# A middle part one step later on ScalarE, a lower part on GpSimd, and GpSimd's constants in another order

## The chip, the cores and the metric

The kernel runs on one core of a Trainium2 chip. A core has five engines that run their own instruction queues and meet only at semaphores: TensorE (PE in the profile, with its weight loads as PEld), VectorE (DVE), ScalarE (ACT), GpSimd (POOL) and SyncE (SP), which here issues nearly all transfers. Work on each engine is done in the order in which the program lists it: an instruction that waits holds up everything behind it on that engine. The metric is the device time of one execution in microseconds (us). Times are given to 0.01 us where they come from the trace.

## The reference: what is computed

Two independent results stand side by side in the output, each of 2048 rows and 576 columns.

The left half is attention with a compressive memory. With `x` of 2048 x 576, the projections `q = x wq`, `k = x wk`, `v = x wv` are cut into 32 heads of 18 columns and four segments of 512 rows. In each segment:

```
logits = qs ks^T * scale + causal mask
a_dot  = softmax(logits) vs
a_mem  = (phi(qs) M) / (phi(qs) z + 1e-6)      phi(t) = t + 1 for t > 0, else exp(t)
o      = g a_mem + (1 - g) a_dot               g = sigmoid(beta), one per head
M += phi(ks)^T vs ;  z += sum of phi(ks)       carried to the next segment
```

The four segments' `o`, put together, are multiplied by `wo`.

The right half is a Fourier mixing layer by matrices: `a = x Hr^T`, `b = x Hi^T` over the 576 columns, and `y = Cr a - Ci b` over the 2048 rows.

## The kernel before, in words

**Numbers in parts.** Products are not made in plain float32. A float32 operand is cut into an upper part (a rounded copy, made by ScalarE) and a lower part (the operand minus its upper part, made by VectorE or GpSimd), and the product is the sum of upper x lower, upper x upper and lower x upper. In the code `split`, `split_wk`, `split_x` and `c_cut` do this. The projected queries and keys are cut into three bfloat16 parts: `p0` is a copy of the PSUM result (ScalarE, L275), `r` the remainder (VectorE, L276), the middle part `p1` a copy of `r` (L285 on GpSimd for the key tiles 5, 6 and 7, L287 on ScalarE for all others) and the last part `p2` the remainder of that (GpSimd, L288).

**Stages.** Stage 1 runs over the four segments (`for s in range(NSEG)`). For each segment it makes nine tiles of 128 rows of projected queries and keys (`project_qk`, in the order m = 0, 1, 2, 3, 8, 4, 5, 6, 7; m = 0 to 3 are queries, 4 to 7 keys, 8 is half and half) and then, for each of four row blocks j, the values (`project_v`). In segments 0 to 2 `project_v` also turns the key tiles by TensorE transposes (`k_natural`, L305) so that they can be summed into the memory (`accumulate`). The transposes read a float32 copy of each key tile, `KF[m]`, which ScalarE makes first thing in `project_qk` (L271). In segments 1 to 3 `lookup` reads the memory. Its last two instructions are VectorE's `w` (L415) and GpSimd's `am` (L417); GpSimd's `vs` (L336) follows. The tiles `am` and `vs` leave by transfers `amd<-am` and `vd<-vs` of SP's queue.

Stage 2 mixes the 32 x 4 attention heads with the Fourier product. `attention()` is a generator of 68 steps (p) of eight slots each. After every slot the loop pulls as many pieces of the generator `dense()` as keep the two in proportion, by given unit costs. `dense()` starts with `hidden`, sixteen products of one chunk of the Fourier input each: `c_load` fetches chunk n to `craw` (four buffers), `c_cut` makes its upper part `chi` and the upper part of its last 128 rows, `xtail`, on ScalarE (L451, L453) and the lower parts `clo` and `xtail` on GpSimd (L456, L458). At the end of the last segment of stage 1 the first two chunks are cut by VectorE instead. Stage 3 is the product with `wo`.

**Order.** What runs when is written out by hand. `later(n, fn)` puts a call off by n ticks, and `tick()` is called after each tile, block or slot. What is due in a tick runs in the order in which it was put off. The middle and last part of a tile are such a call (`rest`), and the transfer of its three parts is put off by one tick more:

```
        def rest():
            if m in (5, 6, 7):
                pool.tensor_copy(p1, r)
            else:
                act.activation(p1, r, AF.Copy)
            pool.tensor_tensor(p2, r, p1, OP.subtract)
            if m < 8:
                later(1, dma, (qd if m < 4 else kd)[s][(m % 4) * P:(m % 4 + 1) * P, :3], p)
```

Buffers matter too. The parts `p` have five buffers, shared with `am`; the remainders `r` have three; a PSUM tile of stage 1 has five. Two TensorE instructions of stage 2 that the change touches by what stands ahead of them are `s` (scores, L965), which needs the PSUM bank that VectorE's row minima (L971) read before, and `trm` (L1022), which turns the row maxima that GpSimd packs into `mb` (L1015 to L1018, `maxima`). `maxima` stands behind the lower part of chunk 5 in GpSimd's order.

**Small tiles.** `attention_constants` makes, on GpSimd, the causal mask (L479, L480), which the row minima read, and clears the two `mb` tiles (L483). `stacks` makes a pair of key and query stacks; its only instruction is GpSimd's memset of ones in the last rows of the key stack (L466). There are four pairs: number 0 is made at the last segment's key tiles, number 1 after j = 1 of its values, and numbers 2 and 3 at the start of attention's steps 0 and 1. `stack_load` fills them by transfers of 432 KB each (`ks<-kd`, `qs<-qd`).

Of the kernel before, what the change touches and what calls it, by code (L numbers as in the profile page):

```python
# [40 lines left out]
def infini_attention_and_fnet(ctx: ExitStack, tc: tile.TileContext, xT, wqk, w8, wv, wo, beta, xtT, cT, hT, out):  # L41
    nc = tc.nc
    act, dve, pool, pe = nc.scalar, nc.vector, nc.gpsimd, nc.tensor
# [44 lines left out]
    def later(n, fn, *a):  # L88
        due.setdefault(clock[0] + n, []).append((fn, a))
# [173 lines left out]
    def project_qk(s, m):  # L263
        if m in FIRST:
            o = FIRST.pop(m)
        else:
            o = ps.tile([P, L], F32, name="qk", tag="acc", bufs=5)
            chain(o, qk_terms(s, m))
        if m >= 4 and s < 3:
            KF[m] = sk.tile([P, L], F32, name="kf", bufs=5)  # L270
            act.activation(KF[m], o, AF.Copy)  # L271
        p = sb.tile([P, 3, L], BF16, name="p", tag="p", bufs=5)
        r = sb.tile([P, L], F32, name="r", tag="r", bufs=3)
        p0, p1, p2 = (p[:, 2 - i] if 4 <= m < 8 else p[:, i] for i in range(3))
        act.activation(p0, o, AF.Copy)  # L275
        dve.tensor_tensor(r, o, p0, OP.subtract)  # L276
        if s and (m < 4 or m == 8):
            n = P if m < 4 else 64
            c = m if m < 4 else 4
            e = sb.tile([P, L], F32, name="qe", bufs=2)[:n]  # L280
            phi(e, ((e, o[:n]),), pq_hi[:n, c], pq_lo[:, c] if m < 4 else pq_hi[64:, c])
# [10 lines that stand above are left out]
                later(1, dma, qd[s][4 * P:, :3], p[:64])  # L292
                for i in range(3):
                    later(1, dma, kd[s][4 * P:, 2 - i], p[64:, i])

        later(1, rest)

    def k_natural(j):
        js = slice(j * P, (j + 1) * P)
# [144 lines left out]
    def c_cut(n, engine=pool):  # L444
        if n < len(CHUNKS):
            raw = c_raw.pop(n)
            hi = sr.tile([P, 4, P], F32R, name="chi", bufs=3)
            lo = sr.tile([P, 4, P], F32R, name="clo", bufs=3)
            t = sr.tile([P, P], F32R, name="xtail", bufs=3) if CHUNKS[n][2] == 5 else None
            c_split[n] = hi, lo, t  # L450
            act.activation(hi, raw[:, :4], AF.Copy)  # L451
            if t is not None:
                act.activation(t, raw[:, 4], AF.Copy)  # L453

            def low():
                engine.tensor_tensor(lo, raw[:, :4], hi.bitcast(F32), OP.subtract)  # L456
                if t is not None:
                    engine.tensor_tensor(t[64:], raw[64:, 4], t[64:].bitcast(F32), OP.subtract)  # L458
            later(1, low)
# [3 lines left out]
    def stacks(p_, i):  # L463
        qs_bufs.append(p_.tile([P, 4, L], BF16, name=f"qs{i}"))
        ks_bufs.append(p_.tile([P, 4, L], BF16, name=f"ks{i}"))
        pool.memset(ks_bufs[i].bitcast(F32)[96:], BF16_ONES)  # L466
# [10 lines left out]
    def attention_constants():  # L477
        t = CAUSAL[0]
        pool.memset(t, 0.0)  # L479
        pool.affine_select(t[:, 384:], t[:, 384:], pattern=[[-1, P]], base=0, channel_multiplier=1,  # L480
                           compare_op=OP.is_ge, fill=LOWEST)
        for m in MB:
            pool.memset(m, 0.0)  # L483
# [16 lines left out]
    for s in range(NSEG):  # L500
        more = s < 3
        if s == 0:
            warm_up()
        open_qk(s)
        if s:
            memory()
        else:
            tick()
        for n, m in enumerate((0, 1, 2, 3, 8, 4, 5, 6, 7)):
            project_qk(s, m)  # L510
            tick()
            if not more and n in (5, 7):
                h_split(0, (n - 5) // 2)
            if s and n < (8 if more else 4):
                copy_parts(s - 1, 2 * n)
                copy_parts(s - 1, 2 * n + 1)
            if s in (1, 2) and n >= 4:
                load_x(s + 1, n - 4)
            if not more and n == 0:
                for k in range(5):  # L520
                    h_load(0, k)
            if not more and n == 4:
                p1k.close()
                sr = ctx.enter_context(tc.tile_pool(name="sb2r", bufs=1, side="right", reuse_waits="tile"))
                attention_tiles()
            if not more and n == 4:
                c_load(0)
                c_load(1)
                stacks(sr, 0)
                stack_load(0)  # L530
            if not more and n == 6:
                c_load(2)
        for j in range(4):
            project_v(s, j, lookup(s, j) if s else iter(()))
            tick()
            for k in ((0, 1), (2, 3), (4,), ())[j] if s == 0 else ():
                load_x(1, k)
            if more and j in (1, 2):
                split_x(s + 1, j - 1)
            if not more and j == 1:  # L540
                stacks(sr, 1)
            if not more and j == 2:
                attention_constants()
            if not more and j == 0:
                h_split(0, 2)
                h_split(0, 3)
            if not more and j == 1:
                h_split(0, 4)
                c_cut(0, dve)
                c_cut(1, dve)  # L550
            if not more and j in (1, 3):
                c_load(3 + j // 2)
            if more and j:
                accumulate(j - 1)
# [393 lines left out]
    sq = ctx.enter_context(tc.tile_pool(name="sb2q", bufs=1, side="right", reuse_waits="tile"))  # L948
# [196 lines left out]
    def attention():  # L1145
        for p in range(NP + V_LAG):
            def even(lag, fn, *a):
                if 0 <= p - lag < NP:
                    fn(2 * (p - lag), *a)

            def odd(lag, fn, *a):
                if 0 <= p - lag < NP:
                    fn(2 * (p - lag) + 1, *a)

            if p < 2:
                stacks(sq, p + 2)
                OG.append(sa.tile([P, 4, 72], F32, name=f"og{p}"))
            if p == 0:
                value_load(0)
                stack_load(1)  # L1160
            if p % 2 == 0:
                later(39, value_load, p // 2 + 1)
                later(30, memory_load, p // 2)
            even(T_LAG + 1, t_lo, 0)
            odd(F_LAG + 1, f_exp, 2)
            odd(F_LAG + 1, f_split_hi)
            yield SLOTS[0]
            G = p // 2 - 1 if p % 2 == 0 and 0 < p <= NP else None
            even(0, s_fill, 0)
            even(T_LAG, t_fill, 0)  # L1170
            even(T_LAG, t_fill, 1, G)
            if G is not None and p < T_LAG:
                maxima_transpose(G, bank("trm", [P, L], F32, "t"))
            odd(F_LAG + 1, f_split_lo, pool, 512, 1280)
            yield SLOTS[1]
            even(0, s_fill, 1)
            odd(F_LAG + 1, f_split_lo, dve, 0, 512)
            yield SLOTS[2]
            even(V_LAG, pv)
            even(0, s_fill, 2)  # L1180
            even(T_LAG, t_mask)
            yield SLOTS[3]
            odd(F_LAG, f_fill, 1)
            even(T_LAG, t_fill, 2)
            odd(F_LAG, f_fill, 0)
            if p % 2 and p < NP:
                maxima(p // 2)
            yield SLOTS[4]
            odd(F_LAG + 1, f_turn)
            if p % 2:  # L1190
                stack_load((p + 3) // 2)
                if p < 16:
                    later(2, copy_parts, 2, 8 + p // 2)
            elif 4 <= p < 36:
                later(2, copy_parts, 3, (p - 4) // 2)
            even(T_LAG, t_hi)
            yield SLOTS[5]
            odd(V_LAG, pv)
            odd(F_LAG, f_fill, 2)
            odd(F_LAG, f_exp, 1)  # L1200
            even(T_LAG, t_lo, 1)
            even(T_LAG, t_lo, 2)
            yield SLOTS[6]
            odd(F_LAG, f_exp, 0)
            if V_LAG <= p < NP + V_LAG - 1:
                pv_out(p - V_LAG)
            yield SLOTS[7]
# [74 lines left out]
```

## Time and profile before

| | |
|---|---|
| median of three runs | 993.6 us (992.38 to 993.71) |
| the profiled execution | 991.08 us, of which 989.4 us are the span of its instructions |
| TensorE busy | 980.1 us, 99% of the span |
| VectorE, ScalarE, GpSimd busy | 790.1 us, 714.6 us, 674.0 us |
| stage 1 | to about 218 us |
| stage 2 (attention and Fourier product) | to about 933 us |

How to read the rows of this profile. A timeline row has the start, the time from the first start to the last end, the engine, the line, the operation, what is written and read, and how many instructions it merges. A bracket at the end gives the engine's idle time just before the row and what ended it. TensorE's matmuls are pipelined and their ends are modelled, so the time that a wait cost TensorE is better read from start to start than from the bracket. In the chain of waits a row has start, length and what the time was spent on. In a table of stretches there is the time, and for each engine its busy time with the number of instructions, then the granted clock, the busy share of the transfer engines and the rate in GB/s.

### The profile page before, as it was taken

Reading aid. Unit: us, or ns where it says so; the run is one execution under the profiler, and the core shown is the slowest. Engines: PE = TensorE matmul, PEld = TensorE weight load, DVE = VectorE, ACT = ScalarE, POOL = GpSimd, SP = SyncE. Lnnn points to the kernel's source line nnn. Section 1 sums busy time; section 2 is a strip of 40 time slices with the busy share of each in tenths; the row PEclk is TensorE's granted clock in tenths of the full one; section 3 lists DMA queues with packets and bytes.
Section 4 is the critical chain, followed back from the end, with each engine's and each line's share of the span. In section 5 each row is a group of like instructions: output and inputs, shape, how many; then the busy total and the mean of one; then the engine's idle time right before and its main releaser. Section 6 shows DMA issues by size and latency. Waiting matters only on the chain.

```text
span 989.4 us, 25491 instructions
## 1 busy us (share of the span) xinstructions
PE 980.1 (99%) x9246; PEld 918.0 (93%) x9246; DVE 790.1 (80%) x2115; ACT 714.6 (72%) x1687; POOL 674.0 (68%) x744
## 2 busy tenths in 40 slices
PE   9999999999999999999999999999999999999998
PEld 8989989898999999999999999999999999999998
DVE  6657668594678787887898887888889899999885
ACT  7757576663888777877878788886777877778442
POOL 2657576686676667676775777767677986667561
PEclk9999999999999999999999999999999999999999
DMA  7537456767577899899999987789999999888663
GB/s 252 188 116 251 185 179 241 238 236 216 147 182 205 225 235 236 199 235 232 226 260 229 236 210 195 183 196 219 234 240 263 229 243 242 206 206 190 168 199 114
DMA packets 304350, 209.96 MB, mean 212 GB/s; under 512 B 204992, under 2 KB 259136, under 8 KB 304192
## 3 DMA queue, kind: packets, MB, share of 16 engines
q1 hardware_dynamic: 304000, 208.20, 80.5%
q8 instruction: 72, 1.18, 0.5%
q14 instruction: 54, 0.44, 0.2%
q10 hardware_dynamic: 224, 0.14, 0.0%
HBM read 122.37 MB, written 58.98 MB: 183 GB/s over the span
## 4 chain that ended last, share of the span: by engine, by line
PE 83%; DVE 8%; ACT 4%; issue 2%; DMA 1%; POOL 1%; SPq 0%; POOLq 0%; DVEq 0%; ACTq 0%
PE d L583 37%; PE s L965 7%; PE v L84 4%; PE pv L1083 4%; PE qk L250 4%; PE d L628 3%; PE d L629 3%; PE d L630 3%; PE t L865 2%; PE pv L1084 2%; PE d L865 2%; PE s L865 1%; PE m L363 1%; PE t L1039 1%; PE qk L84 1%
## 5 line engine op out<-in xcount | busy, mean ns | idle before, releaser
L971 DVE CUSTOM_DVE_ANT_0 s<-s,causal 128x128 f32<-128x128 f32 (+3 forms) x512 | 248.1, 503 | 89.5 <-PE s L965 80.0
L456 POOL TENSOR_TENSOR clo<-craw,chi 128x512 fp32r<-128x512 f32 x158 | 218.0, 1380 | 86.1 <-ACT chi L451 59.6
L583 PE MATMUL d<-wide,chi 128*128 128x288 f32 x1408 | 261.8, 303 | 0.0
L583 PEld LDWEIGHTS d<-wide,chi 128*128 128x128 f32 x1408 | 210.7, 188 | 2.2 <-issue 0.7
L583 PE MATMUL d<-wide,clo 128*128 128x288 f32 x704 | 173.3, 313 | 0.0
L1005 POOL TENSOR_TENSOR hl<-pf,hl 128x768 f16<-128x768 f32 x64 | 112.3, 1755 | 64.5 <-ACT hl L1001 54.6
L1051 ACT ACTIVATE phi<-t 128x384 f16<-128x384 f32 x128 | 61.8, 483 | 102.0 <-PE t L1048 102.0
L965 PE MATMUL s<-ks,qs 108*128 108x128 bf16 (+3 forms) x512 | 132.8, 303 | 2.3 <-DVE negm L971 1.6
L994 ACT ACTIVATE pf<-s,nb 128x128 f32<-128x128 f32 (+3 forms) x256 | 128.3, 527 | 6.2
L1066 DVE TENSOR_TENSOR plo<-pf,phi 128x384 f16<-128x384 f32 (+1 forms) x128 | 128.5, 1004 | 0.0
L583 PE MATMUL d<-ab,chi 128*128 128x288 f32 x640 | 123.3, 302 | 0.0
L583 PEld LDWEIGHTS d<-wide,clo 128*128 128x128 f32 x704 | 117.8, 189 | 1.9 <-issue 0.4
L1052 ACT ACTIVATE pf<-t 128x384 f32<-128x384 f32 (+1 forms) x192 | 99.6, 519 | 6.2 <-PE t L1039 6.0
L451 ACT ACTIVATE chi<-craw 128x512 fp32r<-128x512 f32 x160 | 100.1, 626 | 3.6 <-DMA craw<-xtT 2.0
L583 PEld LDWEIGHTS d<-ab,chi 128*128 128x128 f32 x640 | 97.9, 189 | 0.5
L1001 ACT ACTIVATE hl<-pf 128x768 f16<-128x768 f32 (+1 forms) x128 | 87.4, 729 | 2.0
L583 PE MATMUL d<-ab,clo 128*128 128x288 f32 x320 | 83.0, 308 | 0.0
L628 PE MATMUL d<-wide,chi 128*128 128x288 f32 x256 | 81.4, 318 | 0.0
L630 PE MATMUL d<-wide,clo 128*128 128x288 f32 x256 | 75.6, 295 | 0.9 <-POOL clo L456 0.9
L629 PE MATMUL d<-wide,chi 128*128 128x288 f32 x256 | 75.6, 295 | 0.0
L1066 POOL TENSOR_TENSOR plo<-pf,phi 128x384 f16<-128x384 f32 x64 | 62.4, 974 | 14.9 <-ACT pf L1052 14.5
L1005 DVE TENSOR_TENSOR hl<-pf,hl 128x512 f16<-128x512 f32 x64 | 66.6, 1041 | 0.0
(285 smaller groups left out, 2522.6 us busy)
## 6 DMA issues: line engine op xcount, KB each, us to landing
craw<-cT SPq DMA_DIRECT2D x128, 256.0 KB
ks<-kd SPq DMA_DIRECT2D x32, 432.0 KB
qs<-qd SPq DMA_DIRECT2D x32, 432.0 KB
craw<-xtT SPq DMA_DIRECT2D x32, 320.0 KB
vd<-vs SPq DMA_DIRECT2D x16, 440.0 KB
vst<-vd SPq DMA_DIRECT2D x32, 220.0 KB
qd<-p SPq DMA_DIRECT2D x16, 384.0 KB
kd<-p SPq DMA_DIRECT2D x16, 384.0 KB
```

The lines of the kernel that those rows point to most:

```text
L451: act.activation(hi, raw[:, :4], AF.Copy)
L456: engine.tensor_tensor(lo, raw[:, :4], hi.bitcast(F32), OP.subtract)
L583: pe.matmul(o[h], a, b[:, h * 288:h * 288 + 288], start=start, stop=stop)
L628: pe.matmul(o, xh[:, k], wl[k][:, cs], start=k == 0, stop=False)
L629: pe.matmul(o, xh[:, k], wh[k][:, cs], start=False, stop=False)
L630: pe.matmul(o, xl[:, k], wh[k][:, cs], start=False, stop=False)
L965: pe.matmul(o[:, c:c + w], q[:, i * P:w], k[:, :w], start=True, stop=True)
L971: dve.tensor_tensor_reduce(o[:, c:c + w], o[:, c:c + w], CAUSAL[0][:, L - w:], scale=scale, scalar=-LOWEST, op0=OP.add, op1=OP.min, accum_ ...
L994: act.activation(f[:, FIRST_COL[i]:FIRST_COL[i] + w], o[:, c:c + w], AF.Exp, bias=nb[:, i:i + 1], scale=-1.0)
L1005: engine.tensor_tensor(hl[:, 1, a:b], f[:, a:b], hl[:, 0, a:b], OP.subtract)
L1052: act.activation(f[:, r:r + w], o[:, :w], AF.Exp, bias=LIFT, scale=SCALE)
L1066: (pool if kind == 2 else dve).tensor_tensor(lo[:, a:b], f[:, a:b], hi[:, a:b], OP.subtract)
```

## The change

Four edits. In segments 1 and 2 the middle and last part of key tile 4 (the first key tile proper) are put off by two ticks and not one, so they stand behind the copies of key tile 5. In the last segment `attention_constants` and the second pair of `stacks` change places (j = 1 and j = 2). The lower part of the second Fourier chunk is made by GpSimd and not by VectorE. The pairs 2 and 3 of `stacks` are made in the fourth slot of attention's steps 0 and 1, and not in their first.

```
-        later(1, rest)
+        later(2 if m == 4 and s in (1, 2) else 1, rest)
...
             if not more and j == 1:
+                attention_constants()
+            if not more and j == 2:
                 stacks(sr, 1)
-            if not more and j == 2:
-                attention_constants()
...
             if not more and j == 1:
                 h_split(0, 4)
                 c_cut(0, dve)
-                c_cut(1, dve)
+                c_cut(1, pool)
...
             if p < 2:
-                stacks(sq, p + 2)
                 OG.append(sa.tile([P, 4, 72], F32, name=f"og{p}"))
...
             yield SLOTS[2]
             even(V_LAG, pv)
+            if p < 2:
+                stacks(sq, p + 2)
             even(0, s_fill, 2)
```

More of the change, by code (lines that the diff above doesn't have):

```diff
@@ L294, in rest @@
                     later(1, dma, kd[s][4 * P:, 2 - i], p[64:, i])
-        later(1, rest)
+        later(2 if m == 4 and s in (1, 2) else 1, rest)
     def k_natural(j):
@@ L540, in infini_attention_and_fnet @@
             if not more and j == 1:
+                attention_constants()
+            if not more and j == 2:
                 stacks(sr, 1)
-            if not more and j == 2:
-                attention_constants()
             if not more and j == 0:
@@ L549, in infini_attention_and_fnet @@
                 c_cut(0, dve)
-                c_cut(1, dve)
+                c_cut(1, pool)
             if not more and j in (1, 3):
@@ L1155, in attention @@
             if p < 2:
-                stacks(sq, p + 2)
                 OG.append(sa.tile([P, 4, 72], F32, name=f"og{p}"))
@@ L1179, in attention @@
             even(V_LAG, pv)
+            if p < 2:
+                stacks(sq, p + 2)
             even(0, s_fill, 2)
```

## The prediction

> **What bounds the kernel now.** I read the page first, then the busy time by stretches, then the chain of waits, and last the rows engine by engine where TensorE stands. The last row here is from the table of stretches, the others from the page.
>
> ```profile
> span 989.4 us, 25491 instructions
> ...
> PE 980.1 (99%) x9246; PEld 918.0 (93%) x9246; DVE 790.1 (80%) x2115; ACT 714.6 (72%) x1687; POOL 674.0 (68%) x744
> ...
> PE 83%; DVE 8%; ACT 4%; issue 2%; DMA 1%; POOL 1%; SPq 0%; POOLq 0%; DVEq 0%; ACTq 0%
> ...
> 220.00:240.00 20.00, 17.98 (x133) 17.21 (x131) 10.56 (x36) 7.66 (x20) 11.78 (x16) 1.00 0.75 223
> ```
>
> TensorE is busy for 99% of the span and is 83% of the chain that ended last. Nothing else bounds the kernel for long, so a change gains only what TensorE now waits. In 220 to 240 us, where stage 1 passes into stage 2, it stands 20.00 - 17.98 = 2.02 us, more than in any other stretch of that length before the last one; the change is made around there and at two short waits before it.
>
> The first short waits are those of the transposes in segments 1 and 2 (TensorE's rows; the last one is a row of the chain of waits from a place where nothing was late):
>
> ```profile
> 86.20 0.60 PE L305 MATMUL kt<-ident,kf 128*128 128x128 f32 x4
> 87.00 0.33 PE L305 MATMUL kt<-ident,kf 128*128 128x128 f32 x1 [0.20 <-ACT kf L271]
> 87.31 0.45 PE L396 MATMUL look<-md,pq_hi 128*128 128x152 f32 x2
> ...
> 142.98 0.60 PE L305 MATMUL kt<-ident,kf 128*128 128x128 f32 x4
> ...
> 144.04 0.45 PE L396 MATMUL look<-md,pq_hi 128*128 128x152 f32 x2
> ...
> 163.12 0.55 PE kt L305 x5
> ```
>
> Five transposes and the start of what follows take 87.31 - 86.20 = 1.11 us in segment 1 and 144.04 - 142.98 = 1.06 us in segment 2, where undisturbed ones take 0.55 us: 0.56 + 0.51 = 1.07 us are lost, to ScalarE's copies of the key tiles.
>
> The later waits of TensorE, at the passage:
>
> ```profile
> 221.63 0.38 PE L965 MATMUL s<-ks,qs 108*128 108x128 bf16 x2 [0.31 <-DVE nd L407]
> 223.90 0.27 PE L965 MATMUL s<-ks,qs 108*128 108x256 bf16 x1 [0.83 <-DVE negm L971]
> 229.04 0.41 PE L630 MATMUL d<-wide,clo 128*128 128x288 f32 x1 [0.88 <-POOL clo L456]
> 241.29 0.23 PE L1022 MATMUL trm<-ident,mb 128*128 128x128 bf16 x1 [0.23 <-POOL mb L1018]
> ```
>
> Two of them end with VectorE, two with GpSimd; the brackets of the first three add to the 2.02 us.
>
> **The change part by part.**
>
> *Key tile 4, a step later.* ScalarE in segment 1, with one row each of VectorE (the remainder of tile 6) and GpSimd (last parts of tiles 8 and 4):
>
> ```profile
> 82.47 0.58 ACT L275 ACTIVATE p<-qk 128x512 bf16<-128x512 f32 x1
> 83.88 0.63 ACT L287 ACTIVATE p<-r 128x512 bf16<-128x512 f32 x1 [0.83 <-DVE r L276]
> ...
> 86.32 0.62 ACT L271 ACTIVATE kf<-qk 128x512 f32<-128x512 f32 x1
> ...
> 86.56 0.69 DVE L276 TENSOR_TENSOR r<-qk,p 128x512 f32<-128x512 f32 x1 [0.28 <-ACT p L275]
> ...
> 84.31 2.29 POOL L288 TENSOR_TENSOR p<-r,p 128x512 bf16<-128x512 f32 x2
> ```
>
> The middle part of tile 4 (83.88) waits 0.83 us for its remainder, and behind it stand the copies of tiles 5, 6 and 7, the last at 86.32. From 83.88 to 86.32 there are five starts of 0.49 us each. With the copy and upper part of tile 5 ahead of the middle part, the six starts from 82.47 follow without a gap and the last copy begins at 82.47 + 6 x 0.49 = 85.41. It ends by 86.0; TensorE gets to the fifth transpose at 86.20 + 4 x 0.11 = 86.64. So 0.56 us go here and 0.51 us in segment 2.
>
> What is late next: the lookup after the transposes needs the bank that the remainder of tile 6 reads. That remainder waits for its upper part (now about 85.5) and for the remainder buffer of tile 8, free when GpSimd's first last part ends (84.31 + 1.15 = 85.46). It runs from 85.6 to 86.3; the lookup stands at 86.75. The remainder of tile 7 needs the buffer of tile 4, free at 84.31 + 2.29 = 86.60, and ends near 87.3; the product that needs its bank comes 0.6 us after that. On GpSimd the order stays (tile 4's last part still ahead of tile 5's parts) and the queue is full, so nothing moves. On SP's queue tile 4's transfer is moved past two copies and one load, about 2.2 us; this costs nothing while `am` of the second row block, which takes over the buffer, comes later than the landing (the slower rival). Sum: -1.07 us, bounds -1.07 and 0. I take the first, since every next wait has 0.4 us or more in hand.
>
> All engines of segment 3 start from TensorE's last sums, so I shift them all by 1.07 us up to 216 us.
>
> *The second chunk's lower part, mask and ones.* VectorE, then GpSimd, then SP's transfer, the chain of waits behind it, and who waits for the load:
>
> ```profile
> 216.64 0.68 DVE L456 TENSOR_TENSOR clo<-craw,chi 128x512 fp32r<-128x512 f32 x1
> 217.35 1.15 DVE L458 TENSOR_TENSOR xtail<-craw,xtail 64x128 fp32r<-64x128 f32 x1
> 218.53 1.64 DVE L456 TENSOR_TENSOR clo<-craw,chi 128x512 fp32r<-128x512 f32 x1
> 220.19 0.42 DVE L458 TENSOR_TENSOR xtail<-craw,xtail 64x128 fp32r<-64x128 f32 x1
> 220.63 0.82 DVE L327 TENSOR_TENSOR vr<-v,vs 128x288 f32<-128x288 f32 x2
> ...
> 222.97 0.19 DVE L415 TENSOR_TENSOR w<-look,g 128x32 f32<-128x32 f32 x1
> ...
> 218.31 1.31 POOL L336 TENSOR_TENSOR vs<-vr,vs 128x576 bf16<-128x576 f32 x1
> 219.57 0.52 POOL L479 MEMSET causal<- 128x512 f32 x1
> ...
> 223.30 1.16 POOL L417 TENSOR_TENSOR am<-nd,w 128x576 f32<-128x576 f32 x1 [2.54 <-ACT xtail L453]
> 224.42 1.27 POOL L336 TENSOR_TENSOR vs<-vr,vs 128x576 bf16<-128x576 f32 x1
> 226.68 0.95 POOL L466 MEMSET ks<- 32x1024 f32 x1 [0.99 <-DMA amd<-am]
> 227.72 1.27 POOL L456 TENSOR_TENSOR clo<-craw,chi 128x512 fp32r<-128x512 f32 x1
> 229.07 0.46 POOL L458 TENSOR_TENSOR xtail<-craw,xtail 64x128 fp32r<-64x128 f32 x1
> ...
> 225.71 0.32 SPq L94 DMA_DIRECT2D vd<-vs  x1
> ...
> 228.50 8.99 DMA craw<-xtT
> ...
> 237.58 0.63 ACT L451 ACTIVATE chi<-craw 128x512 fp32r<-128x512 f32 x1 [2.03 <-DMA craw<-xtT]
> ...
> 238.34 1.28 POOL L456 TENSOR_TENSOR clo<-craw,chi 128x512 fp32r<-128x512 f32 x1 [4.00 <-ACT chi L451]
> ```
>
> VectorE loses 220.63 - 218.53 = 2.10 us of work ahead of `vr`. So `vr` begins at 218.5 - 1.07 = 217.45 and `w` ends at 217.45 + (223.16 - 220.63) = 219.98, 3.2 us sooner. The bank of the wait at 221.63 and the minima behind the wait at 223.90 come about as much sooner, TensorE 1.07 and 1.4 us sooner: both waits go. The mask, read by the minima, would now come too late behind the chunk; made before `am` and `vs` of block 2, in the time in which GpSimd made the ones, it is there at 215.5.
>
> GpSimd gets the chunk: after `vs` of block 2 (ends 219.57 - 1.07 = 218.50) come `clo` and `xtail`, 229.07 - 227.72 = 1.35 and about 0.5, so 1.85 us, then the ones of pair 1, 1.0 us, to 221.35. Only then `am` of block 3 can begin, though `w` has been ready since 219.98: it ends at 222.5 and `vs` at 222.5 + 1.27 = 223.77, against 225.69 before. That is 1.92 us sooner, 0.85 more than the shift. Nothing covers these 2.85 us of GpSimd's but the 2.54 us in which it stood idle before 223.30; what is over, 1.37 us past `w`, is paid here. Bounds: VectorE's 1.64 us for the same operation, overlapped with GpSimd's work, shows that the two can hold each other up; were GpSimd's 1.27 stretched as far, 0.4 us of the 1.92 would go. I take 1.27, what GpSimd's own rows have (227.72, 238.34), since VectorE runs `vr` and the lookup's short sums then.
>
> [...]
>
> *The ones of pairs 2 and 3 later.* The memset at 226.68 waits for the landing of `am` and holds up chunk 2's `clo`, for which TensorE waits at 229.04. After the change `clo` follows `vs` at once: 223.8 to 225.1, and TensorE, by then 1.07 + 0.31 + 0.83 = 2.2 us early, asks at about 225.8. The wait goes. The two memsets (0.95 us each) now stand ahead of chunk 3's and chunk 5's lower parts; GpSimd stands idle 4.00 us before the latter (238.34). From chunk 2 to chunk 5 TensorE takes 241.29 - 229.04, or 4.1 us a chunk; it asks for chunk 3 at about 225.8 + 4.1 = 229.9, and GpSimd has it by 225.6 + 0.95 + 1.27 = 227.8. Cost nothing; without that cover 0.95 us each.
>
> *What is late next.* After these, TensorE is 1.07 + 2.02 = 3.09 us early. But at 241.29 it waits for `mb`, which stands in GpSimd's order behind chunk 5, whose upper part waits on ScalarE (237.58) for the load issued at 228.50 and landed 8.99 us later. That load is in SP's queue behind `vd<-vs`, at 225.71 right after `vs`, and behind the loads of a chunk, of values, keys and queries, on transfer engines busy for 0.75 of the stretch. This whole row shifts with `vs`: by 1.92 us and no more. So at `trm` TensorE stands again, 3.09 - 1.92 = 1.2 us longer than the 0.23 us of before, and keeps 1.92 us. From there on every engine is early by the same, and the order of the work does not change.
>
> Sum: -1.07 (transposes) - 0.85 (`vs` of block 3, passed on through the load) = -1.92 us. The profiled execution took 991.08 us and would take 989.16; that execution lies 2.5 us under the median of the three runs, 993.6, so in terms of the median I predict 991.7 us.
>
> **The rivals.**
>
> Full gain: the load of chunk 5 doesn't set the end at `trm`, for instance because it lands sooner when the loads ahead of it are spread. For it speaks that only the last part of that transfer can be as late as 8.99 us; against it that those engines are busy (0.75) and that ScalarE did wait for it (2.03 us). Then all waits go, 1.07 + 2.02 + 0.23 = 3.3 us: 990.3 us.
>
> Half gain: GpSimd loses what VectorE wins, because `clo`, the ones and `am` take 0.85 us longer in their new place. For it speaks that GpSimd has only 2.54 us idle for 2.85 us of work. Then the transposes remain: 992.5 us.
>
> Slower: tile 4's transfer lands late. SP's rows, and `am` of the second row block:
>
> ```profile
> 89.90 0.38 SPq L94 DMA_DIRECT2D kd<-p  x1
> ...
> 91.65 0.62 SPq L109 DMA_DIRECT2D raw<-xT  x1
> 92.38 0.60 SPq L94 DMA_DIRECT2D kd<-p  x1
> ...
> 99.51 1.49 POOL L417 TENSOR_TENSOR am<-nd,w 128x576 f32<-128x576 f32 x1 [1.33 <-ACT xh L59]
> ```
>
> The transfer goes from 89.90 to about 92.0, just ahead of tile 5's. `am` takes its buffer at 99.51 - 0.56 = 98.95. The mechanism decides from a landing later than 6.9 us after the issue; the copies about it in that queue are of a kind that took long above (8.99 us). Each us more holds up GpSimd, the lower part of the keys behind `am` and TensorE's sums. With 2 us in both segments it costs 4 us: 991.7 + 4 = 995.7 us. Against it: the load that now goes ahead of it was itself issued at 91.65 and nothing waited.
>
> **How the numbers follow.** The forecast, gain of 1.92 us less the 0.4 us of the stretched `clo` or plus as much, has 0.60; its own range is 991.2 to 992.2. Full gain 0.20, half gain or none 0.11, slower 0.09. About 0.2%, here 1.99 us, is what a measurement of this kernel can tell from no change, that is 991.6 us. The forecast lies on that bound; the three runs spread over 1.3 us, and the small waits on VectorE in stage 2 can only shrink when work comes sooner, so I give 0.35 of its 0.60 to faster and 0.25 to the same. Faster: 0.35 + 0.20 = 0.55. Same: 0.25 + 0.11 = 0.36. Slower: 0.09. The range from 990.1 (full gain, a little past it) to 993.4 leaves out the slower case, no gain, and the runs beyond the full gain.
>
> **What would show each step.** Right: five transposes of 0.55 us in segments 1 and 2; no 0.83 us before the middle part; `vr` straight behind `xtail` on VectorE; no idle time of TensorE at 221 to 229; `vs` of block 3 about 1.9 us sooner; TensorE's wait for `mb` at `trm` longer by 1.2 us or more. Wrong: `trm` without a wait (full gain), `am` of block 3 no sooner than 1.07 us (half gain), GpSimd waiting for `kd<-p` before `am` (slower).

## The result, and the profile after

The changed kernel takes 989.55 us (median of 14 executions, 987.1 to 992.54), the kernel before 992.46 us (14 executions, 990.45 to 994.17). The ratio is 0.9973, with a 95% interval of 0.9961 to 0.9985: 2.7 us faster, between 1.5 and 3.9. The forecast gain of 1.92 us lies in that interval; the forecast time, 991.7 us with a range down to 990.1, does not fit. One further execution of the changed kernel took 3261.85 us and is left out of every comparison.

The profiled execution of the changed kernel took 992.54 us, the slowest of its 14. By its profile alone the change would look like a loss, and what makes it slow turned out to be the most instructive part of the case. First the head lines of its page (span; busy time, share and instructions of each engine):

```profile
span 990.8 us, 25491 instructions
...
PE 980.7 (99%) x9246; PEld 919.5 (93%) x9246; DVE 785.6 (79%) x2113; ACT 713.9 (72%) x1687; POOL 676.7 (68%) x746
```

VectorE has lost 4.5 us of work and GpSimd gained 2.7 us. TensorE is busy 0.6 us longer with the same 9246 matmuls, which is the first sign that something made matmuls slower.

The timeline of the kernel after, TensorE's rows only (start, length, engine, line, operation, out<-in, count, and idle time with its releaser):

```profile
86.90 0.71 PE L305 MATMUL kt<-ident,kf 128*128 128x128 f32 x5
87.36 0.43 PE L396 MATMUL look<-md,pq_hi 128*128 128x152 f32 x2
...
143.02 0.71 PE L305 MATMUL kt<-ident,kf 128*128 128x128 f32 x5
143.48 0.43 PE L396 MATMUL look<-md,pq_hi 128*128 128x152 f32 x2
...
220.57 0.39 PE L965 MATMUL s<-ks,qs 108*128 108x128 bf16 x2
221.87 0.28 PE L965 MATMUL s<-ks,qs 108*128 108x256 bf16 x1
...
237.51 0.39 PE L965 MATMUL s<-ks,qs 108*128 108x512 bf16 x1
240.76 0.23 PE L1022 MATMUL trm<-ident,mb 128*128 128x128 bf16 x1 [2.86 <-POOL mb L1018]
...
241.54 0.30 PE L630 MATMUL d<-wide,clo 128*128 128x288 f32 x1
241.68 0.30 PE L628 MATMUL d<-wide,chi 128*128 128x288 f32 x1
...
242.20 0.44 PE L628 MATMUL d<-wide,chi 128*128 128x288 f32 x1
242.44 0.44 PE L629 MATMUL d<-wide,chi 128*128 128x288 f32 x1
...
246.38 0.80 PE L965 MATMUL s<-ks,qs 108*128 108x256 bf16 x4
```

and two rows of TensorE before that were not shown, from the same view:

```profile
240.66 0.39 PE L965 MATMUL s<-ks,qs 108*128 108x512 bf16 x1
...
245.37 0.80 PE L965 MATMUL s<-ks,qs 108*128 108x256 bf16 x4
```

Take the same instruction in both timelines and subtract its starts (after less before):

| instruction | before | after | difference |
|---|---|---|---|
| first transpose, segment 1 | 86.20 | 86.90 | +0.70 |
| first lookup, segment 1 | 87.31 | 87.36 | +0.05 |
| first lookup, segment 2 | 144.04 | 143.48 | -0.56 |
| `s`, pair of 108x128 | 221.63 | 220.57 | -1.06 |
| `s`, 108x256 | 223.90 | 221.87 | -2.03 |
| `s`, 108x512, just ahead of `trm` | 240.66 | 237.51 | -3.15 |
| `trm` | 241.29 | 240.76 | -0.53 |
| next four `s` | 245.37 | 246.38 | +1.01 |

The +0.70 is there before any edit acts: by the record of the clock the full clock begins at 6.39 us in this execution and at 4.97 us in the one before, and the first four products (L250) take 1.76 us from first start to last end and not 1.17. From there on the change wins 3.85 us, every wait that it was to remove is gone without a bracket left, and then the whole gain is lost within 9 us. It goes in two steps. First 2.6 us at `trm`: 3.25 us pass from the start of `s` at 237.51 to that of `trm`. Then another 1.5 us although TensorE never stands: at 241.54 one matmul follows the other by 0.14 us, at 242.20 by 0.24 us. The table of stretches of the kernel after, cut at the two moments at which the record of the clock changes there, 241.91 and 245.33, and as far apart on either side, shows why (time, busy time of PE, PEld, DVE, ACT, POOL with counts, granted clock, transfer share, GB/s):

```profile
235.09:238.50 3.41, 2.81 (x21) 2.44 (x19) 0.27 (x1) 1.43 (x4) 0.67 (x1) 1.00 0.90 244
238.50:241.91 3.41, 1.15 (x9) 1.15 (x10) 1.67 (x5) 1.39 (x4) 3.04 (x7) 1.00 0.70 207
241.91:245.33 3.42, 3.42 (x17) 3.27 (x16) 0.00 (x0) 1.13 (x3) 1.12 (x3) 0.50 0.37 107
245.33:248.74 3.41, 3.41 (x26) 3.15 (x25) 3.16 (x13) 0.41 (x1) 1.11 (x2) 1.00 0.56 188
```

After a stretch in which TensorE was busy for 1.15 of 3.41 us, its granted clock is 0.50 for one stretch of the same length: 17 matmuls instead of 26.

The other engines after, answering to the rows shown of before (the timeline again; ScalarE at the key tiles, then the passage):

```profile
84.58 0.63 ACT L287 ACTIVATE p<-r 128x512 bf16<-128x512 f32 x1
...
99.55 1.50 POOL L417 TENSOR_TENSOR am<-nd,w 128x576 f32<-128x576 f32 x1 [0.97 <-DVE w L415]
...
217.94 0.82 DVE L327 TENSOR_TENSOR vr<-v,vs 128x288 f32<-128x288 f32 x2
...
220.27 0.19 DVE L415 TENSOR_TENSOR w<-look,g 128x32 f32<-128x32 f32 x1
...
218.98 1.29 POOL L456 TENSOR_TENSOR clo<-craw,chi 128x512 fp32r<-128x512 f32 x1
...
221.90 1.17 POOL L417 TENSOR_TENSOR am<-nd,w 128x576 f32<-128x576 f32 x1
223.03 1.27 POOL L336 TENSOR_TENSOR vs<-vr,vs 128x576 bf16<-128x576 f32 x1
...
237.83 1.26 POOL L456 TENSOR_TENSOR clo<-craw,chi 128x512 fp32r<-128x512 f32 x1 [5.80 <-ACT chi L451]
...
227.10 2.35 SPq L441 DMA_DIRECT2D craw<-xtT  x3
...
237.07 0.63 ACT L451 ACTIVATE chi<-craw 128x512 fp32r<-128x512 f32 x1 [4.68 <-DMA craw<-xtT]
```

The middle part at 84.58 no longer waits. `vr` follows `xtail` on VectorE, and `vs` of block 3 ends at 224.3; with the late start of 0.70 us taken off that is 223.6, against 223.77 forecast. But chunk 5's upper part on ScalarE begins at 237.07, only 0.51 us sooner than before, so GpSimd stands for 5.80 us and gives `mb` late.

### The profile page after: what moved, and what is told of

Its sections match the earlier page's. It is cut to its first block, busy times and chain, and to the rows that moved or that the text cites. A ratio compares the mean times of both kernels' runs of the same rounds, so it can differ in the third digit from the quotient of the medians.

```text
span 990.8 us, 25491 instructions
## 1 busy us (share of the span) xinstructions
PE 980.7 (99%) x9246; PEld 919.5 (93%) x9246; DVE 785.6 (79%) x2113; ACT 713.9 (72%) x1687; POOL 676.7 (68%) x746
## 4 chain that ended last, share of the span: by engine, by line
PE 92%; DVE 5%; DMA 1%; issue 1%; POOL 0%; ACT 0%; SPq 0%; POOLq 0%; DVEq 0%
PE d L583 38%; PE s L965 7%; PE v L84 6%; PE qk L84 6%; PE qk L250 6%; PE pv L1083 4%; PE d L628 4%; PE d L629 3%; PE d L630 3%; PE pv L1084 2%; PE t L865 1%; PE m L363 1%; PE t L1039 1%; DVE s L971 1%; PE look L396 1%
## 5 line engine op out<-in xcount | busy, mean ns | idle before, releaser
L1066 DVE TENSOR_TENSOR plo<-pf,phi 128x384 f16<-128x384 f32 (+1 forms) x128 | 125.3, 979 | 0.0
```

The lines of the kernel that those rows point to most:

```text
L1066: (pool if kind == 2 else dve).tensor_tensor(lo[:, a:b], f[:, a:b], hi[:, a:b], OP.subtract)
```

## The experiments

Each ratio is to the kernel before on the same chip, with its 95% interval; in us it is the gain of that ratio on 992 us.

**The kernel after again.** No edit; a second profile of the same program.

> The changed kernel, unaltered, beside the other kernels of this series. Theory (the passage's gain is caught again at trm, where TensorE waits for the row maxima behind chunk 5 on GpSimd, and the granted clock falls to half for about 3.4 us where that wait is long): 2 to 3.5 us faster than before, ratio 0.9965 to 0.998; in the profile TensorE waits 2 to 3.3 us before trm, and a half clock behind it in some executions and not in others. Rival (the waits that went are gained in full): 3.6 to 3.9 us faster and no wait before trm.

Measured: 989.63 us (989.49 without the execution of 3261.85 us), ratio 0.9976 (0.9965 to 0.9987), a gain of 2.4 us. Two stretches of this execution:

```profile
236.73:240.15 3.42, 1.64 (x13) 1.27 (x12) 1.66 (x5) 1.27 (x4) 3.05 (x7) 1.00 0.81 221
240.15:243.56 3.41, 3.41 (x17) 3.26 (x16) 0.00 (x0) 1.13 (x3) 1.10 (x3) 0.50 0.47 138
```

and TensorE's rows on its timeline:

```profile
236.84 0.39 PE L965 MATMUL s<-ks,qs 108*128 108x512 bf16 x1
239.01 0.23 PE L1022 MATMUL trm<-ident,mb 128*128 128x128 bf16 x1 [1.78 <-POOL mb L1018]
```

The same picture, with a wait that is 1.1 us shorter and half the clock after it. TensorE is 240.66 - 236.84 = 3.82 us early ahead of `trm`, 241.29 - 239.01 = 2.28 us at `trm`, and 0.75 us after the slow stretch (its four `s` start at 244.62). A mean granted clock of 0.998 or less came in 5 of the 24 executions of this program that are compared: these have a median of 992.2 us, the other 19 of 989.33. (One stretch of 3.41 us at half the clock takes 3.41 x 0.5 / 990 = 0.0017 off the mean.) In the runs of the kernel before that have the clock on record such a mean came once in 90 executions, and in the 22 of the three kernels below with a relief not at all. The half clock is not the rule, but both profiles happened to catch it.

**The first edit alone.**

```
-        later(1, rest)
+        later(2 if m == 4 and s in (1, 2) else 1, rest)
```

> The kernel before with the key tile's middle part a step later, and nothing else. Theory: the 1.1 to 1.3 us of the two transposes' waits are gained, all queues shift alike, so the wait at trm stays 0.4 us and the whole is 1.1 to 1.3 us faster (ratio 0.9987 to 0.9989). Rival (the wait goes, but a queue further on, such as GpSimd's last parts or the transfer moved back on SP, gives it back): within 0.5 us of before.

Measured: 990.1 us, ratio 0.9976 (0.9968 to 0.9985), a gain of 2.4 us (1.5 to 3.2). TensorE's rows:

```profile
86.30 0.71 PE L305 MATMUL kt<-ident,kf 128*128 128x128 f32 x5
86.76 0.43 PE L396 MATMUL look<-md,pq_hi 128*128 128x152 f32 x2
...
220.48 0.38 PE L965 MATMUL s<-ks,qs 108*128 108x128 bf16 x2 [0.31 <-DVE nd L407]
222.75 0.27 PE L965 MATMUL s<-ks,qs 108*128 108x256 bf16 x1 [0.83 <-DVE negm L971]
227.89 0.40 PE L630 MATMUL d<-wide,clo 128*128 128x288 f32 x1 [0.88 <-POOL clo L456]
239.74 0.22 PE L1022 MATMUL trm<-ident,mb 128*128 128x128 bf16 x1
```

The transposes are whole again, the three later waits are untouched to the hundredth, and all rows come 1.15 us sooner (221.63 to 220.48); at `trm` it is 1.55 us, since the 0.23 us wait there is gone as well. That is the forecast term. The medians lie 2.2 us apart (992.32 before on that chip), more than the 1.1 to 1.3 us expected and some 0.7 us more than this profile shows. Single executions scatter by as much (the kernel before again, below), but that is no cause of a difference of medians: what the first edit gains beyond these rows stays open.

**The passage alone**: the kernel after with the first edit undone.

> The changed kernel with the key tile's middle part back in its old place, so the edits at the passage alone. Theory: TensorE gains 2.5 us to 3.2 us on the way to trm and keeps only what chunk 5's load comes sooner, 0.4 to 0.9 us, less where the half clock falls in; ratio 0.9990 to 1.0000. Rival (gained in full): 2.5 us faster or more, ratio below 0.9975.

Measured: 991.05 us, ratio 0.9989 (0.9979 to 0.9998), a gain of 1.1 us (0.2 to 2.1). Its `trm` on the timeline:

```profile
239.55 0.23 PE L1022 MATMUL trm<-ident,mb 128*128 128x128 bf16 x1 [0.18 <-POOL mb L1018]
```

The three other edits gain by themselves, and here `trm` gives almost nothing back: chunk 5 had landed in time. The four `s` behind it start at 243.63, 1.74 us sooner than before, or 2.58 us with this execution's late start of 0.84 us taken off. Up to there this profile is the rival's picture, gained in full; the time is nearer to the theory's, and this execution gives 1.6 us back further on, the largest piece at a wait for `y` (see the kernel before again). The forecast share of these edits was 0.85 us. The first edit alone and the other three alone add to 3.5 us, more than the 2.4 to 2.7 us of all four; the intervals are too wide to make a case of that, but it is what a wait at `trm` that grows with earliness would do.

**The lower part back on VectorE**: the kernel after with one edit undone.

```
-                c_cut(1, pool)
+                c_cut(1, dve)
```

> The kernel after, with the second chunk's lower part back on VectorE; the other three edits stay. Theory (that edit frees TensorE of the waits of 0.31 and 0.83 us at the scores and brings `vs` of block 3 forward by 0.85 us beyond the shift of edit 1): `vr` of block 3 begins some 2 us later than in the kernel after, TensorE's two waits at the scores are back with 0.4 and 0.9 us or so, and the time is about 0.9 us above the kernel after, some 990.4 us, ratio 0.998 to 0.999. Rival (whatever is won ahead of the row maxima is waited for there, since chunk 5 lands when it lands): the two waits are back, the wait at `trm` is shorter by the same, and the time is that of the kernel after within 0.4 us, some 989.5 us.

Measured: 990.31 us, ratio 0.9985 (0.9975 to 0.9994), 0.8 us above the kernel after. TensorE's rows:

```profile
220.61 0.38 PE L965 MATMUL s<-ks,qs 108*128 108x128 bf16 x2 [0.17 <-DVE nd L407]
222.88 0.27 PE L965 MATMUL s<-ks,qs 108*128 108x256 bf16 x1 [0.83 <-DVE negm L971]
...
238.73 0.22 PE L1022 MATMUL trm<-ident,mb 128*128 128x128 bf16 x1
```

Both waits on VectorE are back and the median is the theory's. In this one profile `trm` does not wait, which is the rival's mechanism at work in a single execution; the medians differ by less than their intervals, so this run favours the theory and does not prove it.

**The ones early again**: the kernel after with the two memsets back in the first slot.

```
             if p < 2:
+                stacks(sq, p + 2)
                 OG.append(sa.tile([P, 4, 72], F32, name=f"og{p}"))
...
-            if p < 2:
-                stacks(sq, p + 2)
             even(0, s_fill, 2)
```

> The changed kernel with the ones of pairs 2 and 3 back at the start of attention's steps 0 and 1. Theory (what TensorE gains ahead of trm it loses there): TensorE waits again about 1 us for chunk 2 and as much less before trm, so the time is that of the changed kernel within 0.5 us, with fewer half clocks. Rival (that edit's gain counts by itself): 1 us slower than the changed kernel, ratio to before 0.9985.

Measured: 990.85 us, ratio 0.9988 (0.998 to 0.9997), 1.3 us above the kernel after. TensorE's rows:

```profile
227.38 0.40 PE L630 MATMUL d<-wide,clo 128*128 128x288 f32 x1 [1.49 <-POOL clo L456]
...
240.16 0.23 PE L1022 MATMUL trm<-ident,mb 128*128 128x128 bf16 x1 [0.78 <-POOL mb L1018]
```

The wait for chunk 2's lower part is back, at 1.49 us and not 0.88, because TensorE now comes to it sooner. The time is the rival's: it rises, and the wait is not merely exchanged for a shorter one at `trm`. But the two intervals overlap (0.998 to 0.9985), and in this profile the four `s` behind `trm` start 1.13 us sooner than before, sooner than in either profile of the kernel after. So the run favours that the third edit counts for itself and does not prove it.

**The maxima ahead of chunk 5**: `maxima(0)` of step 1 moved in front of chunk 5's lower part on GpSimd.

```
             even(0, s_fill, 2)
+            if p == 1:
+                maxima(0)
...
-            if p % 2 and p < NP:
+            if p % 2 and 1 < p < NP:
                 maxima(p // 2)
```

> The changed kernel with the packing of the first group's row maxima on GpSimd ahead of chunk 5's lower part and not behind it. Theory: trm doesn't wait any more; TensorE waits for chunk 5 itself instead, about 1 to 1.5 us, so 1.5 to 2 us of the 3.2 are gained, and the half clock goes with the long wait: 1.5 to 2.5 us faster than the changed kernel, ratio to before 0.994 to 0.996. Rival (the wait before trm was no cost to the end, or chunk 5's load holds up TensorE as long): within 0.7 us of the changed kernel.

Measured: 988.07 us (5 executions), ratio 0.9959 (0.9946 to 0.9973). ScalarE's and TensorE's rows on the timeline:

```profile
237.19 0.63 ACT L451 ACTIVATE chi<-craw 128x512 fp32r<-128x512 f32 x1 [4.95 <-DMA craw<-xtT]
...
237.58 0.22 PE L1022 MATMUL trm<-ident,mb 128*128 128x128 bf16 x1
...
238.86 0.40 PE L628 MATMUL d<-wide,chi 128*128 128x288 f32 x1 [1.06 <-DVE wide L94]
```

`trm` does not wait any more, which shows that the order on GpSimd made that wait. The load is as late as ever: ScalarE, held up 4.95 us by it, is late with the sums of the product before, VectorE's lower part of them (`wide`) comes later still, and TensorE stands 1.06 us a little further on. The wait is smaller, and no half clock follows: the matmuls behind it stay 0.13 to 0.14 us apart (239.46, 239.59, 239.73).

**The first load of values a step later**: what stands next to chunk 5's load in SP's queue is moved out of its way.

```
             if p == 0:
-                value_load(0)
                 stack_load(1)
+            if p == 1:
+                value_load(0)
```

> The changed kernel with the first load of values (220 KB) issued one attention step later, so that it no longer stands ahead of chunk 5's load in SP's queue. Theory (chunk 5's landing sets the time at trm): the load lands about 0.8 to 1.0 us sooner, the wait before trm shrinks by as much, the half clock gets rarer: 0.8 to 1.5 us faster than the changed kernel, ratio to before 0.9955 to 0.9970. Rival (the landing is set by all that is in flight, not by what stands ahead): within 0.4 us of the changed kernel.

Measured: 987.88 us (5 executions), ratio 0.9962 (0.995 to 0.9974). SP's, ScalarE's and TensorE's rows:

```profile
226.10 0.96 SPq L441 DMA_DIRECT2D craw<-xtT  x2
...
233.78 0.63 ACT L451 ACTIVATE chi<-craw 128x512 fp32r<-128x512 f32 x1 [1.77 <-DMA craw<-xtT]
...
237.12 0.39 PE L965 MATMUL s<-ks,qs 108*128 108x512 bf16 x1
237.50 0.23 PE L1022 MATMUL trm<-ident,mb 128*128 128x128 bf16 x1
```

Chunk 5's load is issued 1.00 us sooner than in the kernel after and its upper part begins 3.29 us sooner. `trm` follows `s` by 0.38 us; TensorE is 3.79 us early at `trm` and keeps it (its four `s` start at 241.59, 3.78 us before those of the kernel before).

**The same again**, on another chip.

> The kernel after, with the first load of values issued at attention's step 1, unaltered from the run before of that name. Theory (a long wait at `trm` takes back what the passage gained, and now and then halves the clock; without it both are gone): ratio 0.9955 to 0.9970, no execution at a granted clock of 0.998 or less, the wait at `trm` below 0.6 us. Rival (its 988 us were a lucky set of five): at 989 to 990 us, ratio 0.997 to 0.998, like the kernel after.

Measured: 988.91 us (7 executions), ratio 0.997 (0.9959 to 0.9981). Neither expectation fits fully: the ratio is at the upper end of the theory's, and the time at the lower end of the rival's. The mechanism is confirmed by its table of stretches, in which the passage has no idle time of TensorE left:

```profile
220.00:240.00 20.00, 20.00 (x153) 19.43 (x152) 8.59 (x28) 8.03 (x22) 14.85 (x20) 1.00 0.76 242
```

All 12 executions of this program together have a median of 988.4 us, about 1 us below the 989.55 us of the kernel after. With the two other kernels that relieve `trm` it is the best found, and its advantage over the kernel after is about what separates two sets of its own.

**Both reliefs** (the maxima ahead and the values later).

> The changed kernel with both reliefs: the row maxima packed ahead of chunk 5 and the first load of values a step later. Theory: the wait left in maxima_first (TensorE waits 1.1 us for VectorE's lower part, which is late because ScalarE waits for chunk 5's load) goes too: 0.5 to 1.1 us faster than maxima_first, ratio to before 0.9945 to 0.9955. Rival (nothing is left to gain at the passage): the same as maxima_first, 0.9959.

Measured: 988.28 us (5 executions), ratio 0.9963 (0.9951 to 0.9975): no better than either alone, as the rival had it. Its profile has no idle time of TensorE left from 220 to 240 us, so the 1.06 us that the maxima alone left is gone there; the medians of five do not show it, and why stays open.

**The values later in the kernel before.**

> The kernel before, with only the first load of values issued at attention's step 1 and not at step 0 (the edit that took the wait at `trm` from the kernel after). Theory (that load only matters by what it holds up: chunk 5, for which TensorE waits 0.23 us in the kernel before): TensorE gains no more than 0.3 us, ratio 0.9995 to 1.0005; chunk 5's upper part comes 1.5 to 3 us sooner, and the waits at 221 to 229 us stay. Rival (the load's place is worth something by itself, which would be part of what the kernel with all four edits and this one gained): 1 us or more faster, ratio below 0.999.

Measured: 991.89 us, ratio 1.0 (0.9991 to 1.0009): the theory's zero. If the move is worth anything, it is so only after the change, when TensorE comes early. Whether chunk 5 landed sooner stays unclear: its upper part begins at 236.01 here, 1.57 us sooner than in the first profile of the kernel before, but in the next run, without the move, it begins at 236.36, and that execution runs 0.3 us later throughout.

**The kernel before again**, as a kernel of its own.

> The kernel before, unaltered, as a kernel of its own: what two sets of runs of the same program differ by. Expected: ratio 1.0000 within 0.0008. If its profiled execution shows the transposes of segments 1 and 2 at 1.1 us and the waits of 0.31, 0.83 and 0.88 us again, those are fixed by the order of the work; if the kernel with the first edit alone gained 2.2 us by chance, this row's scatter has to be near 1 us.

Measured: 991.99 us, ratio 1.0003 (0.9994 to 1.0011). Its profiled execution took 991.77 us, 0.7 us more than the one that the prediction was made from, with the same waits of 0.31, 0.83 and 0.88 us; 0.5 us of it are at the start, before any edit acts. So the rows quoted are fixed by the order of the work, and a profile's total is not: the first profile of the kernel before was 1.4 us below the 992.46 us of its own median. Two places that no edit touches make part of this scatter. One is the start: the first transposes of segment 1 come at 86.20 us in the first profile of the kernel before, in which the full clock begins at 4.97 us, at 86.90 in that of the kernel after, in which it begins at 6.39, and at 87.04 with the passage alone. The other lies far behind the passage: in five of the 14 profiles, that of the run before this one among them and both of the kernel before not, TensorE waits 1.0 us for VectorE's `y`, as here in the kernel after again:

```profile
759.61 0.53 PE L583 MATMUL d<-wide,chi 128*128 128x288 f32 x2 [1.02 <-DVE y L653]
```

So what one profile shows of a stage is worth more than its total.

**Chunk 5's load behind chunk 6's**, to make the wait longer.

```
-        c_load(n + 4)
+        if n != 1:
+            c_load(n + 4)
+        if n == 2:
+            c_load(5)
```

> The changed kernel with chunk 5's load issued behind chunk 6's. Theory: it lands 1 to 1.5 us later, the wait before trm grows from 2 to 3.3 us to 3.5 to 4.5 us, and the half clock falls in nearly every execution (mean granted clock 0.998 or less) and costs about 1.5 us each: 1.5 to 3 us slower than the changed kernel, near the kernel before. Rival (the half clock has another cause than that wait): slower by the 1 to 1.5 us alone, with the half clock in a fifth of the executions as now.

Measured: 990.47 us, ratio 0.9986 (0.9976 to 0.9996). The expected lateness failed to come: chunk 5 landed 8.8 us after its issue, no later than in the kernel after. So this run says little on the load. Two of its 12 executions (993.19 and 993.76 us) have a mean granted clock of 0.998, no more often than in the kernel after. But it holds a long wait with the full clock behind it (stretches of this run, cut every 3.41 us; `trm` waits 2.69 us from start to start, 237.88 to 240.57, across a cut):

```profile
235.82:239.24 3.42, 2.45 (x18) 2.07 (x16) 0.82 (x2) 2.38 (x7) 1.54 (x2) 1.00 0.87 276
239.24:242.65 3.41, 2.08 (x16) 2.08 (x17) 1.12 (x3) 0.33 (x2) 2.68 (x7) 1.00 0.39 131
242.65:246.06 3.41, 3.41 (x27) 3.08 (x26) 2.23 (x10) 1.54 (x4) 1.75 (x2) 1.00 0.56 194
```

A longer wait than the 2.17 us of the kernel after again, and no half clock.

## Why the prediction was right or wrong

**Key tile 4** (forecast -1.07 us): right. In the kernel after the first lookup follows the first transpose by 0.46 us in both segments; before by 1.11 and 1.06 us. That makes -1.25 us. The term was 0.18 us too small because the undisturbed length was read as 0.55 us from the chain of waits, in which the last transpose's full length is counted; start to start it is 0.46. With this edit alone the later waits stand as they were. The slower rival is refuted by the row at 99.55: `am` waits for VectorE's `w` and not for a transfer.

**The second chunk's lower part** (forecast: both waits at the scores go, `vs` 1.92 us sooner): right, as far as it goes. GpSimd's 1.29 us for the chunk is the 1.27 us taken, not the 1.64 us of the bound. Half gain is refuted: `am` of block 3 begins 1.40 us sooner, 2.1 with the late start taken off.

**The ones later** (forecast: the wait goes, the cover holds): right in the rows; with the memset at the old place the median is 1.3 us higher, with intervals that overlap.

**The size of the waits** was a mis-sized term: 0.31 + 0.83 + 0.88 = 2.02 us were brackets. From start to start the three waits were worth 0.50, 0.97 and 1.12 us (-0.56 to -3.15 in the table), 2.59 us. The part ahead of the prediction says that a wait is better read from start to start, and the sum used the brackets all the same.

**What is late next** named the right place and the wrong rule. `trm` became the one wait, behind chunk 5's load, as forecast. But "this whole row shifts with `vs`: by 1.92 us and no more" failed as a rule: `trm` came 1.23 us sooner in one profile of the kernel after (0.53, with the late start of 0.70 added) and 2.28 us in the other. The issue did move as forecast: chunk 5's load left 1.40 and 2.06 us sooner in the two profiles, 2.10 and 2.05 with the difference of their starts taken out. The landing did not follow it. In the profiles with the values at step 0, it was issued at 227.10 and 226.44 in the kernel after, 226.94 with the maxima first and 227.36 with the first edit alone, and ScalarE had it at 237.07, 235.28, 237.19 and 235.79. 1.92 us is a fair middle for something that scatters by 2 us. And the step ended at the wait, where the time did not: in both profiles of the kernel after the wait is followed by 3.41 us at half the clock, 1.5 us more, and 5 of its 24 executions, these two among them, have a mean clock of 0.998 or less. No term of the sum, and no rival, stood for that.

**The number** failed at the last step, "in terms of the median". The forecast 989.16 us for one execution was raised by the 2.5 us between the profiled execution and a median of three, 993.6 us; fourteen executions have 992.46. The term was 1.38 us (992.46 - 991.08) and not 2.5, and that is 1.1 of the 2.15 us by which 991.7 was too high. With 1.38 us the same sum gives 990.5 us, and a range that begins at 989.0. The rest, 1.0 us, is gain: 2.9 us between the two medians for 1.92 forecast. The undersized terms give 0.75 us of earliness (0.18 + 0.57), and `trm` lets some of it through, more in executions in which chunk 5 lands early, as with the passage alone. How much it lets through in the 19 executions with an undisturbed clock was not seen, since both profiles of this program caught the other kind; that stays open. So it is in part luck that the forecast gain of 1.92 us lies in the measured interval: the waits were worth more than the sum had, and `trm` takes back a share that differs from execution to execution. About the full gain of 3.3 us is what the kernel with the values later shows (3.8 and 3.0 us by its two ratios).

## What to carry to other kernels

When several small waits go at once, look for the next place at which the bound engine meets another one, and ask how long it will stand there in one piece: here one wait of 3.25 us from start to start took back 2.6 us, and 3.41 us at half the clock behind it another 1.5, more than the 2.59 us of the three waits that it replaced. Size waits from start to start, and put a predicted gain against many executions, not against a median of three. A transfer behind others in a loaded queue is better given by a range of landings, here 7.2 to 10.3 us, than shifted with its issue.

## What was not expected of the hardware

**Half the clock after a wait of 2 us.** In the records of the first profiles of the two kernels the granted clock changes only at multiples of 3.413 us from the moment at which it is first full, 4.97 us in the kernel before and 6.39 us in the kernel after: after, it is full from 6.39 to 241.91, 69 such stretches, half for one, and full again for 218; before, it is full for 288, to 988.01. What goes with it is TensorE's idle share of one such stretch: 0.66 (1.15 us busy of 3.41) and, in the kernel after again, 0.52 (1.64 of 3.42) were followed by a stretch at 0.50; 0.28 and 0.39, the two parts of the wait of 2.69 us as cut above, were not. Nor was the 0.26 of the stretch that holds the wait at 229.04 in the kernel before (its table of stretches):

```profile
226.84:230.25 3.41, 2.54 (x19) 2.30 (x19) 0.59 (x2) 0.77 (x3) 3.17 (x4) 1.00 1.02 281
```

That is the largest share of its 287 stretches ahead of the last one; in the kernel after the largest that was followed by the full clock is 0.18 (2.81 us busy of 3.41, from 235.09). At the ends of the two programs, where the work runs out, a stretch of 0.85 (before, 0.50 us busy of 3.41, from 984.60) and one of 0.89 (after, 0.36 of 3.41, from 986.02) were followed by 0.50. In the stretch at 0.50 of the kernel after, the chunk's matmuls follow one another by 0.24 us (242.20 to 242.44), ahead of it by 0.14 (241.54 to 241.68). The waits of 3.25 and 2.17 us at `trm` were followed by half the clock and by 1.5 us more; the wait of 2.69 us, which runs across a cut, was not. That its place among the stretches decides, and not its length, is the author's estimate from these three waits; what decides between shares of 0.39 and 0.52 was not shown.

**Landing times.** In the profiles of kernels with the values' load at step 0, ScalarE had chunk 5 from 7.2 us (228.59 to 235.81, the passage alone) to 10.3 us (226.94 to 237.19, the maxima first) after its issue, and an earlier issue did not bring an earlier landing. With that load a step later, in the order of the kernel after, it took 7.1 to 7.9 us in three profiles and began at 233.00 to 234.11; the earliest of the others is 234.96 (the lower part back on VectorE). In the kernel before the same move changed nothing in the time (ratio 1.0, 0.9991 to 1.0009). Whether, and how, the neighbours in the queue delay a load was not settled.
